# Loading q in 1 KB pieces, transposing it head by head, and reordering the first loads of an attention + FFN kernel

## The chip, the cores and the metric

The kernel runs on one core of a Trainium2 chip. The metric is the device time of one execution in microseconds. Three runs of the kernel before gave 884.79, 886.57 and 888.91 us, a median of 886.57 us.

## What is computed

The inputs are q, k and v of 8 batches, 8 heads, 576 positions and 64 features, a gain `g_norm` of 64 values, and two weight matrices of 512 x 2048 and 2048 x 512, which arrive as 64-bit floats.

```
kv  = einsum('bhsd,bhse->bhde', k, v)            # a 64 x 64 matrix for each batch and head
out = einsum('bhsd,bhde->bhse', q, kv)
x   = out / sqrt(mean(out*out, -1) + 1e-6) * g_norm   # rows: 4608 tokens, columns: 8 heads x 64
h   = x @ w_in
g   = h * tanh(log1p(exp(min(h, 20))))           # for h > 20: h * tanh(h)
result = g @ w_out                               # 4608 x 512
```

## The kernel before, in words

The 4608 tokens are nine tiles of 512. Because a batch has 576 positions, tile 0 lies in batch 0 alone, tile 1 takes 64 tokens of batch 0 and 448 of batch 1, and so on; `segments(j)` gives the pieces of a tile. In a first part each tile goes through attention and the first matrix product, and its result is stored to DRAM (`gd`); in a second part this is loaded again and multiplied with `w_out`. Both products use a seven-product scheme on 2 x 2 blocks (`PROD`), each operand as a high and a low half in a short float type, so that one product is a run of 12 matmul instructions (L527 in the first part, L772 in the second).

**Weights.** The 64-bit `w_in` is loaded in eight pieces of 1 MB, called `weights(0)` to `weights(7)`, each by two transfers (L137). A piece has to be turned into halves before a product can use it, in steps that the code names: `SCALE` (ScalarE, L142), `JOIN` (VectorE, three operations L147 to L149), `DIFF` (VectorE, L157 to L159), `BLOCKS` and `SUMS` (a cast on ScalarE, L121, and a subtraction on VectorE, L122). The raw words wait in a room that is free again after `JOIN`: pieces 0, 4 and 7 share the room `w64`, pieces 2 and 5 the room `wf6`, pieces 3 and 6 the room `wf7`.

**Attention.** For batch 0, k and v come in two halves of four heads each (L226, `kv_first`) and are multiplied in `kv_first_product` (L234). For every later batch k and v come in four parts of two heads (`k_load(b, 0)` to `k_load(b, 3)`, four transfers each: `km`, `kr`, `vm`, `vr`, L213 and L214), and `k_product(b, p)` (L252) multiplies them; only two parts have a place to land at once, so part 2 can be sent for once the product of part 0 is done. `kv_keep` copies the result out of PSUM (ScalarE, L269 and L274; VectorE, L276). A tile's heads are worked in two units of four heads. For tiles 0 and 1 a unit is: `transpose` q on TensorE (L325), copy it out (`turned`, L338 or L336), `project` with kv (L360), `square` (L370, L373), `scaled` (L378, from tile 1 on, with the gain `gcol`), `sums` (L391, L399), `rstd` (L408, L409 for tile 0) and `normalize` (L430, with `gcol`). For later tiles VectorE transposes.

**What sets the order.** The order on each engine is that of the program text; nothing is rearranged. The first tile is written out line by line. From then on a table orders the work: a step of the table, a slot, is one product of 12 matmuls, and `at(n, ...)` hangs other work behind the product of slot n. All loads and nearly all stores are issued by one engine, SyncE (SP), in program order, and an issue waits until its room is free; what stands behind it waits too. SP also keeps at most eight transfers under way: each issue waits for the landing of the one eight places earlier. After slot 0's work come, in the table: `weights(6, LOAD)` and `weights(3)` at slot 1 and `k_load(1, 2)` behind them; `k_load(1, 3)` at slot 2; `weights(4, SCALE)` and the other steps of piece 4 from slot 4; `kv_keep(1)` at slot 4; `project` of tile 1 at slots 5 and 11; the second `transpose` of tile 1 at slot 8.

Of the kernel before, what the change touches and what calls it, by code (L numbers as in the profile page):

```python
# [8 lines left out]
F32 = mybir.dt.float32  # L9
# [18 lines left out]
def linear_attention_rms_mish_ffn(  # L28
# [49 lines left out]
    G = 2 * P  # L78
# [4 lines left out]
    TR = T // P  # L83
# [11 lines left out]
    att = part1.enter_context(tc.tile_pool(name="att", bufs=1))  # L95
# [132 lines left out]
    def kv_first_product(n):  # L228
        kt, vt = kv0
        for hp in range(n.start, n.stop):  # L230
            for c in range(9):
                for o in range(2):
                    r, d = slice(o * D, (o + 1) * D), slice(c * D, (c + 1) * D)
                    nc.tensor.matmul(kvps[r, 0, hp, :], kt[r, hp, d], vt[r, hp, d], start=(c == 0), stop=(c == 8))  # L234
# [21 lines left out]
    kvf, kvt = [], []  # L256
# [9 lines left out]
    def kv_keep(b, n):  # L266
        for r in (slice(0, D), slice(D, P)):
            if b < T32:
                nc.scalar.copy(kvf[b][r, n, r], kvps[r, b % 2, n, :])  # L269
        if b < T32 - 1:  # L270
            return
        t = kvt[b % 2]
        for r in (slice(0, D), slice(D, P)):
            nc.scalar.copy(t[r, 0, n, r], kvps[r, b % 2, n, :])  # L274
        for r in (slice(0, D), slice(D, P)):
            nc.vector.tensor_sub(t[r, 1, n, r], kvps[r, b % 2, n, :], t[r, 0, n, r].bitcast(F32))  # L276


    def segments(j):

        n = (S - T) * j
        segs = []
        if n:
            segs.append((j - 1, S - n, slice(0, n)))
        if n < T:
            segs.append((j, 0, slice(n, T)))
        return segs

    def rows_load(j, c):
        for b, s0, cols in segments(j):  # L290
            t0, t1 = max(cols.start, c * P), min(cols.stop, (c + 1) * P)
            if t0 < t1:
                src = q[b, 0:1, s0 + t0 - cols.start:s0 + t0 - cols.start + 1, :]
                src = bass.AP(src.tensor, src.offset, [[D, t1 - t0], [S * D, H], [1, D]])
                nc.sync.dma_start(rows[j][t0 - c * P:t1 - c * P, c, :].rearrange("p (h d) -> p h d", d=D), src)

    rows = {}
    qs, ss = {}, {}

    def unit_steps(j, u):  # L300
        st = {}
# [13 lines left out]
        def transpose():  # L315
            if j < T32:
                if j == 0 and u == 1:
                    ps = [bank_new("a").rearrange("p m t -> p (m t)") for _ in range(2)]
                else:
                    x2 = ps_t.tile([P, 2, T], F32, name="x2")  # L320
                    ps = [x2[:, a] for a in range(2)]
                for a in range(2):
                    h = 4 * u + 2 * a
                    for c in range(TR):
                        nc.tensor.transpose(ps[a][:, c * P:(c + 1) * P], rows[j][:, c, h * D:(h + 2) * D], ident)  # L325
                st["ps"] = ps if j == 0 and u == 1 else x2
                return
            t = st["q"] = att.tile([P, 2, T], F32, name="fl")
            src = qs[u].rearrange("p a (c d) -> p (a c) d", d=D)[:, :, 0:R]
            nc.vector.transpose(t.rearrange("p a (c d) -> p (a c) d", d=R), src)  # L330
# [19 lines left out]
        def project():  # L350
            if j == 0 and u == 1:
                st["x"] = [bank_new("a").rearrange("p m t -> p (m t)") for _ in range(2)]
            else:
                x2 = st["x2"] = ps_t.tile([P, 2, T], F32, name="x2")
                st["x"] = [x2[:, a] for a in range(2)]
            for a in range(2):
                ps, hp = st["x"][a], 2 * u + a
                for b, _, c in segments(j):
                    if j < T32:
                        nc.tensor.matmul(ps[:, c], kvf[b][:, hp, :], st["q"][:, a, c], start=True, stop=True)  # L360
                        continue
                    kh, kl, qh, ql = kvt[b % 2][:, 0, hp, :], kvt[b % 2][:, 1, hp, :], st["qh"][:, a, c], st["ql"][:, a, c]
                    nc.tensor.matmul(ps[:, c], kl, qh, start=True, stop=False)
                    nc.tensor.matmul(ps[:, c], kh, ql, start=False, stop=False)
                    nc.tensor.matmul(ps[:, c], kh, qh, start=False, stop=True)
# [60 lines left out]
        def normalize():  # L426
# [39 lines left out]
    def bank_new(name):  # L466
        return ps_m.tile([P, 2, TH], F32, name=name)
# [3 lines left out]
    def at(t, f):  # L471
        plan.setdefault(t, []).append(f)
# [86 lines left out]
    def do(j, u, *steps):  # L559
        for s in steps:  # L560
            units[j][u][s]()
# [19 lines left out]
    def k_load(b, p):  # L581
        staged[b, p] = kv_load(nc.sync, b, 2 * p, 2, kv_staging())
# [5 lines left out]
    nc.scalar.preload_act_table_set("natural_log_exp_and_others")  # L588
    weights(0, LOAD)
    t = wfp.tile([P, 3, 2 * T], F32, name="wf2")  # L590
    rows[0], turned_q = t[:, 0:2].rearrange("p a (c n) -> p (a c) n", c=TR // 2), t[:, 2].rearrange("p (a t) -> p a t", a=2)
    for c in range(TR):
        rows_load(0, c)
    kv0 += [wfp.tile([P, NKC, 9 * D], F32, name=f"wf{n}") for n in (3, 4)]
    kv_first(first)
    weights(1, LOAD)
    kv_first(second)
    for r in (slice(0, D), slice(D, P)):
        nc.sync.dma_start(gcol[r, :], g_norm.rearrange("(p o) -> p o", o=1))
    weights(2, LOAD)  # L600
    weights(4, LOAD)
    weights(3, LOAD)
    make_identity(nc, ident)
    kv_tiles()
# [11 lines left out]
    do(0, 1, "transpose")  # L616
    weights(0, BLOCKS)
    do(0, 0, "turned")
    weights(0, SUMS)
    do(0, 1, "turned")  # L620
    weights(1, SCALE, JOIN)
    kv_first_product(first)
    kv_keep(0, first)
    do(0, 0, "project", "square")
    weights(1, DIFF, BLOCKS)
    kv_first_product(second)
# [4 lines left out]
    do(0, 0, "rstd")  # L631
    k_load(1, 0)
    k_load(1, 1)
    rows[1] = att.tile([P, TR, H * D], F32, name="qs")
    for c in range(TR):
        rows_load(1, c)
    do(0, 1, "square", "sums")
    weights(2, SCALE)
    do(0, 0, "normalize")
# [2 lines left out]
    do(0, 1, "rstd", "normalize")  # L642
    x_form(S1)
    weights(2, DIFF)
    weights(5, LOAD)


# [3 lines left out]
    for j in range(3, NF2):  # L651
        t = 3 * (j - 3) + 1
        if j < 5:
            at(t, lambda j=j: weights((6, 7)[j - 3], LOAD))
        for s, n in ((SCALE, 0), (JOIN, 0), (DIFF, 1), (BLOCKS, 1), (SUMS, 2)):
            at(t + n, lambda j=j, s=s: weights(j, s))

# [6 lines left out]
    for b in range(2, B):  # L664
        t = NS * (b - 2)
# [117 lines left out]
    def o_store(st):  # L783

        i, half = divmod(st["s"], T // G)
        if i < T32:
            for r in range(G // P):
                c = half * G // P + r
                for b, s0, cols in segments(i):
                    t0, t1 = max(cols.start, c * P), min(cols.stop, (c + 1) * P)  # L790
                    if t0 < t1:
                        row = b * S + s0 + t0 - cols.start
                        nc.sync.dma_start(out[row:row + t1 - t0, :], st["o"][t0 - c * P:t1 - c * P, r, :])
# [43 lines left out]
    t = NS * NT  # L837
# [13 lines left out]
    st = gs[0]  # L851
    for n in range(NF2 // 2):
        if n + 1 < NF2 // 2:
            g_pair(st, n + 1, pair_rooms(n + 1))
        for c in range(2):
# [3 lines left out]
            for (left, right), (b, h) in where.items():  # L859
                gf = st["f"][left, n]  # L860
                for s, (a, d) in enumerate(((1, 0), (0, 1), (0, 0))):
# [3 lines left out]
                        start=n == c == s == h == 0, stop=last_one, skip_group_check=True,  # L865
# [87 lines left out]
```

## Time and profile before

| quantity | value |
|---|---|
| median of 3 runs | 886.57 us |
| the profiled execution's own time | 885.97 us |
| its span, first to last instruction | 884.2 us |
| TensorE (PE) busy | 828.1 us, 94% |
| VectorE (DVE) busy | 608.7 us, 69% |
| ScalarE (ACT) busy | 464.6 us, 53% |
| PE busy in the first 54 us | 24.14 us |
| PE busy from 54 to 97 us | 39.84 of 43 us |

The page of the profile cuts the span into 40 slices of 22.1 us; a digit is the busy share in tenths. A timeline row has the start, the time from the start of the first to the end of the last instruction of the row, the engine (SPq is the queue in which SP issues transfers), the line, the operation, the tiles written and read, shapes and the count; in brackets the idle time before it and what ended that. A 32-bit float matmul shows as two matmul instructions, a transpose as one. The chain of waits follows the work that ended last back through what released it.

### The profile page before, as it was taken

Reading aid. Unit: us, or ns where it says so; the run is one execution under the profiler, and the core shown is the slowest. Engines: PE = TensorE matmul, PEld = TensorE weight load, DVE = VectorE, ACT = ScalarE, POOL = GpSimd, SP = SyncE. Lnnn points to the kernel's source line nnn. Section 1 sums busy time; section 2 is a strip of 40 time slices with the busy share of each in tenths; the row PEclk is TensorE's granted clock in tenths of the full one; section 3 lists DMA queues with packets and bytes.
Section 4 is the critical chain, followed back from the end, with each engine's and each line's share of the span. In section 5 each row is a group of like instructions: output and inputs, shape, how many; then the busy total and the mean of one; then the engine's idle time right before and its main releaser. Section 6 shows DMA issues by size and latency. Waiting matters only on the chain.

```text
span 884.2 us, 17156 instructions
## 1 busy us (share of the span) xinstructions
PE 828.1 (94%) x7036; PEld 795.7 (90%) x7036; DVE 608.7 (69%) x804; ACT 464.6 (53%) x703; POOL 4.8 (1%) x23
## 2 busy tenths in 40 slices
PE   4658998998999999999999899999999999999997
PEld 3447898998999999999999789999999999999997
DVE  5869675886777676787764368867777677776772
ACT  3647666556675765666664444344444434434431
POOL 2000000000000000000000000000000000000000
PEclk9969999999999999999999999999999999999999
DMA  9936787987978696767477993344434443334421
GB/s 294 247 114 197 200 274 246 278 263 226 296 219 278 218 304 199 220 204 227 151 227 249 425 416 125 122 150 152 148 121 133 130 120 120 119 120 141 153 65 48
DMA packets 161038, 175.52 MB, mean 199 GB/s; under 512 B 24704, under 2 KB 142464, under 8 KB 159936
## 3 DMA queue, kind: packets, MB, share of 16 engines
q1 hardware_dynamic: 158208, 170.23, 61.8%
q10 hardware_dynamic: 2752, 4.20, 1.3%
q8 instruction: 55, 0.90, 0.4%
q14 instruction: 23, 0.19, 0.1%
HBM read 112.39 MB, written 62.00 MB: 197 GB/s over the span
## 4 chain that ended last, share of the span: by engine, by line
PE 63%; DMA 11%; DVE 10%; ACT 9%; issue 4%; SPq 2%; ACTq 0%; DVEq 0%
PE a L772 22%; PE bc L772 16%; PE a L527 13%; PE bc L527 7%; DMA gd<-ula 5%; PE s L252 2%; DMA vm<-in_v_dram 2%; DVE ur L548 1%; DMA wod<-wst 1%; ACT L412 1%; ACT gf L121 1%; DMA rd<-fl 1%; DVE gf L122 1%; DVE fa L122 1%; ACT L118 1%
## 5 line engine op out<-in xcount | busy, mean ns | idle before, releaser
L772 PE MATMUL a<-wf,gf 128*128 128x256 f32 x1632 | 201.8, 283 | 0.5 <-DVE ur L812 0.5
L772 PEld LDWEIGHTS a<-wf,gf 128*128 128x128 f32 x1632 | 198.4, 192 | 0.7 <-DVE ur L812 0.7
L122 DVE TENSOR_TENSOR gf<-g,gf 128x1024 fp32r<-128x1024 f32 (+1 forms) x123 | 132.9, 1087 | 90.7 <-ACT gf L121 90.7
L527 PE MATMUL a<-gf,wf 128*128 128x256 f32 x1296 | 173.0, 287 | 11.5 <-DVE gf L430 4.5
L527 PEld LDWEIGHTS a<-gf,wf 128*128 128x128 f32 x1296 | 162.9, 193 | 18.1 <-ACT ur L504 6.6
L527 PE MATMUL bc<-gf,wf 128*128 128x256 f32 x1296 | 170.3, 285 | 3.5 <-ACT ur L495 2.4
L527 PEld LDWEIGHTS bc<-gf,wf 128*128 128x128 f32 x1296 | 161.4, 191 | 5.1 <-ACT ur L495 2.6
L121 ACT CAST gf<-g 128x1024 fp32r<-128x1024 f32 (+1 forms) x123 | 114.6, 939 | 93.3 <-DVE g L752 65.1
L772 PE MATMUL bc<-wf,gf 128*128 128x256 f32 x1224 | 152.7, 283 | 1.0 <-DVE gf L122 1.0
L772 PEld LDWEIGHTS bc<-wf,gf 128*128 128x128 f32 x1224 | 149.4, 192 | 1.4 <-ACT gf L121 0.7
L527 PE MATMUL a<-a,wf 128*128 128x256 f32 x432 | 59.8, 289 | 2.5 <-DVE ur L548 2.5
L527 PEld LDWEIGHTS a<-a,wf 128*128 128x128 f32 x432 | 55.8, 195 | 5.6 <-DVE ur L548 3.1
L118 ACT ACTIVATE ur<-ur 128x1024 f32<-128x1024 f32 x36 | 38.1, 1059 | 37.1 <-DVE ur L548 37.1
L122 DVE TENSOR_TENSOR fa<-fl,fh 128x1024 fp32r<-128x1024 f32 x28 | 34.3, 1224 | 22.1 <-ACT fh L121 21.2
L504 ACT COPY ur<-a 128x512 f32<-128x512 f32 (+1 forms) x53 | 27.3, 516 | 37.6 <-PE a L772 24.6
L122 DVE TENSOR_TENSOR gf<-gf 128x512 fp32r<-128x512 f32 x45 | 30.4, 689 | 24.0 <-ACT gf L121 24.0
L121 ACT CAST gf<-a 128x1024 fp32r<-128x1024 f32 x17 | 17.9, 1052 | 53.5 <-DVE a L749 50.9
L121 ACT CAST gf<-gf 128x512 fp32r<-128x512 f32 x45 | 27.1, 618 | 31.4 <-DVE gf L451 19.1
L495 ACT COPY ur<-bc 128x512 f32<-128x512 f32 (+1 forms) x53 | 27.4, 517 | 29.9 <-PE bc L772 23.0
L548 DVE TENSOR_TENSOR ula<-bc,ula 128x512 f32<-128x512 f32 x36 | 24.8, 688 | 25.4 <-PE bc L527 25.3
L118 ACT ACTIVATE ula<-ula 128x512 f32<-128x512 f32 x36 | 22.8, 633 | 22.1 <-DVE ula L548 22.1
L252 PE MATMUL s<-vm,km 128*64 128x64 f32 x448 | 20.1, 235 | 14.1 <-DMA vm<-in_v_dram 14.1
(137 smaller groups left out, 858.1 us busy)
## 6 DMA issues: line engine op xcount, KB each, us to landing
g<-gd SPq DMA_DIRECT2D x18, 2048.0 KB, 8.9
gd<-ur SPq DMA_DIRECT2D x32, 512.0 KB, 4.0
wod<-wst SPq DMA_DIRECT2D x16, 896.0 KB, 5.6
wf<-wod SPq DMA_DIRECT2D x8, 1792.0 KB, 16.2
gd<-ula SPq DMA_DIRECT2D x32, 256.0 KB, 5.1
gd<-ulb SPq DMA_DIRECT2D x32, 256.0 KB, 4.3
w<-in_moe_w_out_dram SPq DMA_DIRECT2D x32, 256.0 KB, 4.6
km<-in_k_dram SPq DMA_DIRECT2D x28, 256.0 KB, 4.8
```

The lines of the kernel that those rows point to most:

```text
L118: nc.scalar.activation(o, i, AF.Mish)
L121: nc.scalar.copy(hi, src)
L122: nc.vector.tensor_sub(lo, src, hi.bitcast(F32))
L252: nc.tensor.matmul(kvps[o * D:(o + 1) * D, b % 2, h0 // 2 + i, :], kt, vt, start=(c == 0), stop=(c == CM))
L412: nc.scalar.preload_act_table_set("natural_log_exp_and_others")
L495: then(t + 2, lambda: nc.scalar.copy(dst(st, "22"), st["c"]))
L504: then(t + 4, lambda: nc.scalar.copy(dst(st, "12"), st["a"]))
L527: nc.tensor.matmul(bank[:, jj], w[:, right, a, kc, :], xf[:, b, kc, :], start=first and jj == kc == s == 0, stop=(kc == 1 and s == 2), ski ...
L548: nc.vector.tensor_add(o, bank, o)
L772: nc.tensor.matmul(bank, gf[:, a, c, :], wo[c][:, right, b, :], start=first and c == s == 0, stop=(c == NF2 - 1 and s == 2), skip_group_ch ...
```

## The change

- q of tiles 0 and 1 is laid out anew: partition p holds tokens 4p to 4p+3 of the tile (before: p, 128+p, 256+p, 384+p), head by head, so that a contiguous piece in DRAM is 1 KB and no longer 256 bytes. Tile 0 needs one transfer of 1 MB (before four of 256 KB), tile 1 needs two (before five).
- The transposes of tiles 0 and 1 take one head at a time: 16 ordinary 32-bit matmuls against the identity for each unit, 128 x 64 stationary, the two heads of a pair into the two halves of the output partitions (before: 8 transposes of 128 x 128, two heads at once).
- In `project` of tile 1 the columns of a batch are now 16 or 112 in each of four groups of 128, read and written with that stride.
- The loads of later weights move: `weights(4, LOAD)` from before `weights(3, LOAD)` to the end of the first tile's text, in front of `weights(5, LOAD)`; `weights(6, LOAD)` and `weights(7, LOAD)` by two slots, behind `k_load(1, 2)` and `k_load(1, 3)`.
- `gcol` is loaded by GpSimd's queue (before by SP's).
- In the first tile's text `kv_first_product(first)` and `kv_keep(0, first)` come ahead of `weights(1, SCALE, JOIN)`, and the second unit's copy of the turned q ahead of `weights(0, SUMS)`.
- The stores of the result of tiles 0 and 1 follow the new token order: one transfer for each batch and half tile, 4 KB pieces.

```
@@ rows_load
+    def spots(cols):
+        return slice(cols.start // TR, cols.stop // TR)
-    def rows_load(j, c):
+    def rows_load(j):
         for b, s0, cols in segments(j):
-            t0, t1 = max(cols.start, c * P), min(cols.stop, (c + 1) * P)
-            if t0 < t1:
-                src = q[b, 0:1, s0 + t0 - cols.start:s0 + t0 - cols.start + 1, :]
-                src = bass.AP(src.tensor, src.offset, [[D, t1 - t0], [S * D, H], [1, D]])
-                nc.sync.dma_start(rows[j][t0 - c * P:t1 - c * P, c, :].rearrange("p (h d) -> p h d", d=D), src)
+            p = spots(cols)
+            src = q[b, 0:1, s0:s0 + 1, :]
+            src = bass.AP(src.tensor, src.offset, [[TR * D, p.stop - p.start], [S * D, H], [1, TR * D]])
+            nc.sync.dma_start(rows[j][p], src)
@@ transpose
-                    h = 4 * u + 2 * a
                     for c in range(TR):
-                        nc.tensor.transpose(ps[a][:, c * P:(c + 1) * P], rows[j][:, c, h * D:(h + 2) * D], ident)
+                        for o in range(2):
+                            src = rows[j][:, 4 * u + 2 * a + o, c * D:(c + 1) * D]
+                            nc.tensor.matmul(ps[a][o * D:(o + 1) * D, c * P:(c + 1) * P], src, ident, start=True, stop=True)
@@ project
-                        nc.tensor.matmul(ps[:, c], kvf[b][:, hp, :], st["q"][:, a, c], start=True, stop=True)
+                        o, r = (t.rearrange("p (c n) -> p c n", n=P)[:, :, spots(c)] for t in (ps, st["q"][:, a]))
+                        nc.tensor.matmul(o, kvf[b][:, hp, :], r, start=True, stop=True)
@@ the first tile's text
-    for c in range(TR):
-        rows_load(0, c)
+    rows_load(0)
...
-        nc.sync.dma_start(gcol[r, :], g_norm.rearrange("(p o) -> p o", o=1))
+        nc.gpsimd.dma_start(gcol[r, :], g_norm.rearrange("(p o) -> p o", o=1))
     weights(2, LOAD)
-    weights(4, LOAD)
     weights(3, LOAD)
...
     do(0, 0, "turned")
+    do(0, 1, "turned")
     weights(0, SUMS)
-    do(0, 1, "turned")
-    weights(1, SCALE, JOIN)
     kv_first_product(first)
     kv_keep(0, first)
+    weights(1, SCALE, JOIN)
...
-    for c in range(TR):
-        rows_load(1, c)
+    rows_load(1)
...
     weights(2, DIFF)
+    weights(4, LOAD)
     weights(5, LOAD)
@@ the table
         if j < 5:
-            at(t, lambda j=j: weights((6, 7)[j - 3], LOAD))
+            at(t + 2, lambda j=j: weights((6, 7)[j - 3], LOAD))
```

The order on SP, in the rows that follow the loads of tile 1's q (`qs`). `wf_387` is weights(5) and `wf_441` weights(6) before; `w_394` is weights(4), `wf_397` weights(5) and `wf_540` weights(6) in the change. Before:

```order
L295 DMA qs<-in_q_dram 128x8x64 x3
L137 DMA wf_387<-in_moe_w_in_dram 128x4x256 x2
L137 DMA wf_441<-in_moe_w_in_dram 128x4x256 x2
L213 DMA km<-in_k_dram 128x2x256
L214 DMA kr<-in_k_dram 64x2x64
L213 DMA vm<-in_v_dram 128x2x256
L214 DMA vr<-in_v_dram 64x2x64
```

In the change:

```order
L298 DMA qs<-in_q_dram 112x8x256
L137 DMA w_394<-in_moe_w_in_dram 128x4x256 x2
L137 DMA wf_397<-in_moe_w_in_dram 128x4x256 x2
L213 DMA km<-in_k_dram 128x2x256
L214 DMA kr<-in_k_dram 64x2x64
L213 DMA vm<-in_v_dram 128x2x256
L214 DMA vr<-in_v_dram 64x2x64
L213 DMA km<-in_k_dram 128x2x256
L214 DMA kr<-in_k_dram 64x2x64
L213 DMA vm<-in_v_dram 128x2x256
L214 DMA vr<-in_v_dram 64x2x64
L137 DMA wf_540<-in_moe_w_in_dram 128x4x256 x2
```

weights(6) now stands behind all eight transfers of batch 1's third and fourth parts, and weights(4) and weights(5) stand ahead of them.

The order on ScalarE in the first tile's text, from the copy of the first turned q on (`wf_217`/`wf_227` are weights(0) as halves, `wf_148`/`wf_145` the raw words of weights(1), `kvf` the kept kv of batch 0). Before:

```order
L338 COPY fh<-x_198 128x1024
L121 CAST wf_217<-wd 128x4x256
L142 ACTIVATE fl<-wf_148 128x1024
L269 COPY kvf_168<-s_123 64x2x64 x2
L370 ACTIVATE fa<-x_271 128x1024
```

In the change:

```order
L342 COPY fh<-x_192 128x1024
L121 CAST wf_227<-wd 128x4x256
L269 COPY kvf_162<-s_123 64x2x64 x2
L142 ACTIVATE fl<-wf_145 128x1024
L375 ACTIVATE fa<-x_281 128x1024
```

The copies of the first kv product moved ahead of the scaling of weights(1).

More of the change, by code (lines that the diff above doesn't have):

```diff
@@ L590, in linear_attention_rms_mish_ffn @@
     t = wfp.tile([P, 3, 2 * T], F32, name="wf2")
-    rows[0], turned_q = t[:, 0:2].rearrange("p a (c n) -> p (a c) n", c=TR // 2), t[:, 2].rearrange("p (a t) -> p a t", a=2)
-    for c in range(TR):
-        rows_load(0, c)
+    rows[0], turned_q = t[:, 0:2].rearrange("p a (h n) -> p (a h) n", h=H // 2), t[:, 2].rearrange("p (a t) -> p a t", a=2)
+    rows_load(0)
     kv0 += [wfp.tile([P, NKC, 9 * D], F32, name=f"wf{n}") for n in (3, 4)]
@@ L633, in linear_attention_rms_mish_ffn @@
     k_load(1, 1)
-    rows[1] = att.tile([P, TR, H * D], F32, name="qs")
-    for c in range(TR):
-        rows_load(1, c)
+    rows[1] = att.tile([P, H, TR * D], F32, name="qs")
+    rows_load(1)
     do(0, 1, "square", "sums")
@@ L786, in o_store @@
         if i < T32:
[L787 to L793, printed above, removed]
+            for b, s0, cols in segments(i):
+                p = spots(cols)
+                row = b * S + s0 + half * G // P
+                dst = out[row:row + 1, :]
+                dst = bass.AP(dst.tensor, dst.offset, [[TR * DM, p.stop - p.start], [DM, G // P], [1, DM]])
+                nc.sync.dma_start(dst, st["o"][p])
             return
```

## The prediction

> **What bounds the kernel now.** I read the page first, then the list of waits, then the timelines of the engines that these name.
>
> ```profile
> span 884.2 us, 17156 instructions
> PE   4658998998999999999999899999999999999997
> PEclk9969999999999999999999999999999999999999
> km<-in_k_dram SPq DMA_DIRECT2D x28, 256.0 KB, 4.8
> ```
>
> TensorE is busy nine tenths from the fifth slice on; whatever the change gains or loses there is its own work. The room is in the first three slices (4, 6, 5), 66 us, where all edits lie but the stores. Who waits for whom from 54 us on, and then SP's, ScalarE's and VectorE's timelines:
>
> ```profile
> PE s L252 <- DMA vm<-in_v_dram: 12.9, 1, 12.9
> ```
>
> ```profile
> 35.19 12.57 SPq L137 DMA_DIRECT2D wf<-in_moe_w_in_dram  x4
> 47.86 0.45 SPq L213 DMA_DIRECT2D km<-in_k_dram  x1
> 49.06 0.59 SPq L213 DMA_DIRECT2D vm<-in_v_dram  x1
> ```
>
> ```profile
> 50.31 1.04 ACT L121 CAST wf<-wd 128x1024 fp32r<-128x1024 f32 x1
> 59.05 0.58 ACT L504 COPY ur<-a 128x512 f32<-128x512 f32 x1 [7.70 <-PE a L527]
> 59.53 1.12 ACT L142 ACTIVATE fl<-w 128x1024 f32<-128x1024 f32 x1
> 70.58 1.11 ACT L378 ACTIVATE gf<-x,gcol 128x1024 f32<-128x1024 f32 x1
> ```
>
> ```profile
> 32.29 1.23 DVE L149 SCALAR_TENSOR_TENSOR fl<-wf,fl 128x1024 uint32<-128x1024 uint32 x1
> 51.73 1.22 DVE L122 TENSOR_TENSOR wf<-wd,wf 128x1024 fp32r<-128x1024 f32 x1
> 60.69 0.69 DVE L147 TENSOR_SCALAR fl<-fl 128x1024 uint32<-128x1024 uint32 x1 [7.74 <-ACT fl L142]
> ```
>
> TensorE stands 12.9 us for part 2 of batch 1's k and v. SP is held from 35.19 to 47.76 by four issues, of weights(5) and weights(6); the latter waits for a room that VectorE's third join of weights(3) frees. Only then are k and v sent for. But VectorE and ScalarE used that time: they converted weights(3) until 51.73 + 1.22 = 52.95 and 50.31 + 1.04 = 51.35. Their own loss is 7.74 and 7.70 us. And the next stretch is theirs:
>
> ```profile
> 58.95 0.69 PE L252 MATMUL s<-vm,km 128*64 128x64 f32 x16
> 62.78 2.12 PE L360 MATMUL x<-fh,kvf 128*128 128x64 f32 x8
> 71.75 1.22 PE L325 MATMUL x<-ident,qs 128*128 128x128 f32 x8 [2.54 <-ACT gf L378]
> 72.62 2.91 PE L527 MATMUL a<-a,wf 128*128 128x256 f32 x12
> 77.52 1.69 PE L527 MATMUL a<-gf,wf 128*128 128x256 f32 x12
> ```
>
> At 71.75 TensorE waits once more, 2.54 us, for ScalarE's L378, which ends a chain of conversions that began with the scaling of weights(4) at 59.53. So what reaches the end is how much earlier that scaling starts, not how long TensorE stood.
>
> **The change part by part.**
>
> *Moved loads: +7.70 us.* weights(4) needs nothing (its room's first tenant is joined by then) and weights(5) waits for the third join of weights(2), 32.29 + 1.23 = 33.5. Part 2 then waits for its place, that is for the product of part 0 (36.47 + 1.12 in a row below, with the rest by 37.9), and not for 47.86. Its four issues take 0.45 to 0.60 each, so vm is issued near 39.1 and, with 4.8 us to landing as on the page, is there by 43.9. Part 3 follows the product of part 1 (its last start near 40.5): issued 40.8 to 43, there by 47. TensorE then does part 2 (1 us), the third product (1.6, or 2.9 at the slow clock) and is done by 47.7 at the latest. ScalarE wants this product at 51.35. So its whole wait of 7.70 goes, with 3.6 us in hand; `kv_keep(1)` wants part 3's product near 53, with 4 us in hand. What is late next is ScalarE itself: TensorE will stand for `kv_keep` and then again for L378, some 3 us each. Less than 7.70 comes out only if part 2 lands after 47.5. Weights(4) to (7) land later than now, but weights(4) is wanted at 51, weights(5) near 60; weights(6) is issued after the third join of weights(3) as now, weights(7) after that of weights(4) as now: nothing.
>
> *Start: +0.85 us.* Here are the rows, DMA stretches first (the last number is GB/s), then TensorE, ScalarE and VectorE.
>
> ```profile
> 0.00:4.00 4.00, 0.00 (x0) 0.00 (x0) 0.00 (x0) 1.28 (x1) 3.40 (x12) 1.00 0.47 143
> 6.00:9.00 3.00, 0.72 (x2) 0.36 (x2) 1.47 (x2) 1.12 (x1) 0.00 (x0) 1.00 1.39 219
> 20.00:24.00 4.00, 4.00 (x77) 2.74 (x76) 3.86 (x7) 2.61 (x6) 0.00 (x0) 1.00 1.09 356
> ```
>
> ```profile
> 12.11 1.91 PE L325 MATMUL a<-ident,wf 128*128 128x128 f32 x8
> 14.35 2.39 PE L234 MATMUL s<-wf,wf 64*64 64x64 f32 x72 [0.32 <-DMA wf<-in_v_dram]
> 24.89 1.88 PE L360 MATMUL a<-wf,kvf 128*128 128x512 f32 x4
> 36.47 1.12 PE L252 MATMUL s<-vm,km 128*64 128x64 f32 x16
> ```
>
> ```profile
> 17.32 1.12 ACT L142 ACTIVATE fl<-wf 128x1024 f32<-128x1024 f32 x1 [3.01 <-DMA wf<-in_moe_w_in_dram]
> 18.34 0.51 ACT L269 COPY kvf<-s 64x128 f32<-64x128 f32 x2
> 23.75 1.05 ACT L121 CAST wf<-wd 128x1024 fp32r<-128x1024 f32 x1
> ```
>
> ```profile
> 22.90 0.42 DVE L159 TENSOR_TENSOR wd<-fl,wd 128x256 f32<-128x256 f32 x1
> 27.21 1.41 DVE L430 SCALAR_TENSOR_TENSOR gf<-x,gcol,fa 128x512 f32<-128x512 f32 x2 [1.15 <-ACT fa L409]
> ```
>
> The 256-byte pieces of q move at 219 GB/s, larger ones at 356. weights(0) and q are 2.1 MB; at 356, from about 2.4 us (0.57 MB by 4.0), they are in at 8.3, when the transposes begin; the first k and v (1.2 MB) follow by 11.7 and no longer set the start of their product.
>
> The new transposes do. Their price is in no row; the nearest is L252, also 128 x 64 stationary with alternating output halves. With a last instruction of 0.22 (0.31 slow) its 16 start every (0.69 - 0.22)/15 = 31 ns, (1.12 - 0.31)/15 = 54 ns at the slow clock. L360 streams 512 columns in (1.88 - 0.59)/3 = 0.43 us, 54 ns for 64: so two halves overlap in L252. Twice the columns make 62 ns (slow 108) if they overlap here too, 108 (slow 215) if not. I take the overlap. The instruction lengths show which clock holds when:
>
> ```profile
> L325 PE MATMUL a<-ident,wf x8: 421/421/422, 12.1 to 13.6; 128*128 128x128 f32 x8
> ```
>
> ```profile
> L325 PE MATMUL x<-ident,qs x16: 272/273/404, 40.6 to 72.6; 128*128 128x128 f32 x16
> ```
>
> ```profile
> L360 PE MATMUL a<-wf,kvf x4: 592/593/593, 24.9 to 26.2; 128*128 128x512 f32 x4
> ```
>
> ```profile
> 31.60:35.00 3.40, 0.77 (x6) 0.77 (x7) 3.33 (x5) 0.32 (x1) 0.00 (x0) 1.00 0.86 193
> 35.10:38.40 3.30, 3.30 (x29) 2.84 (x29) 3.20 (x7) 0.62 (x1) 0.00 (x0) 0.50 1.28 221
> 72.60:75.90 3.30, 3.30 (x16) 2.74 (x14) 3.16 (x7) 2.25 (x6) 0.00 (x0) 0.50 0.58 162
> ```
>
> TensorE is slow up to 14.5, and stretches of 3.4 us are slow after one in which it stood (0.77 busy, then 0.50). Of 64 transposes from 8.3, if the clock lifts at 12.0, 34 run slow and 30 fast: done at 13.9. If it lifts at 11.1, 13.5; at 14.6, 15.0. The Trainium skill (TensorE: Matmul & The Clock Gate, section "What's actually happening") calls the activity window free-running, so that the count of slow matmuls changes from run to run; by it any point from 13.5 to 15.0 is as good.
>
> The first kv product (2.39) ends at 16.3, its copies (0.51, now ahead of weights(1)) at 16.9. L142 starts there, not at 17.32, and VectorE's L159 ends 6.0 later (22.90 + 0.42 - 17.32), at 22.9. The cast that now starts at 23.75, held by the copies of the second kv product, starts with it: 0.85 us earlier (1.35 to -0.15), and all up to 51.35 is in order behind it. The second product is no brake: project at 17.0, then 1.9 and 2.3, ends at 21.2.
>
> *Transposes in tile 1: -1.1 us.* The first unit's lie in front of part 2's landing and cost nothing; without that cover, 1.1. The second unit's begin when L378 lets them: 32 x 62 ns = 2.0 in place of 72.62 - 71.75 = 0.87. From there TensorE is the bound. The slow stretch after the standing (2.91 for a product that takes 1.69 otherwise) is there now and will be again; bounds -0.6, and -2.6 without overlap.
>
> The Trainium skill (TensorE: Matmul & The Clock Gate, section "Measured speedup vs the span model") gives three column tiles 2.38 times one, an efficiency of 0.79. For two that is an estimate of 1.6 times, 68 ns in place of 62: start and second unit would lose 0.4 together, sum 7.0. L252's own 54 against 31 is 1.74 times, and I keep it.
>
> *At nothing.* `gcol` by GpSimd: first read by L430 at 27.21, some 20 us after GpSimd is free; if it held the identity beyond 8.3, the start would pay. The strided columns of `project` are as many as now (2.12 us for eight; at worst again as much in each unit, mostly covered). Stores of tiles 0 and 1: fewer issues on SP in the second part, behind TensorE. q of tile 1 now follows the first two parts directly behind weights(3), 1 MB earlier in the queue, and is wanted only behind the product of part 1.
>
> **Sum**: 7.70 + 0.85 - 1.1 = 7.45. The profiled execution took 885.97, so 878.5; it lies 0.6 below the median of 886.57, so I leave it at that. Its own range is 876.8 to 880.5.
>
> **Rivals.**
>
> *The output halves do not overlap.* 17 slow and 47 fast of 108 ns end at 17.1; the cast slips 2.2, the second unit costs 2.6: 7.70 - 4.8 = 2.9, 883.1. For it: these are full-height weights and twice L252's columns; against it L252.
>
> *Slower: they neither overlap nor wake the clock.* The place is the start and the second unit. 64 x 215 ns end at 22.1, the cast at 31.0 (7.2 late), the second unit pays 6.0: 885.97 + 5.5 = 891.5. It decides from 157 ns for an instruction on, where 96 of them eat the 7.70. For it: the slow clock held up to 14.5 although transposes ran since 7.6. Against it: it lifted at the end of an unbroken stretch of them.
>
> *The load does not come earlier*, because SP is held at weights(5) or by its limit of eight as long as now: only the other terms stay, 885.97 - 0.85 + 1.1 = 886.2. Against it: the third join of weights(2) ends at 33.5.
>
> *More*: the clock lifts at 11.1 and the slow stretch of 2.91 against 1.69 falls elsewhere, 0.5 + 1.2 more: 876.8 or a little less.
>
> **How the numbers follow.** Forecast 0.62, no overlap 0.11, slower 0.05, load not earlier 0.08, more 0.14. A measurement tells some 0.5%, 4.4 us, from no change. Forecast and more are faster beyond that: 0.76. No overlap (3.5 below the median) and the late load are within it: 0.19. Slower: 0.05. The range 874.5 to 884.0 takes in the first, second and last case and leaves out 0.13 and some tail.
>
> **What would show it.** Right: no wait of L252 over 2 us near 42; ScalarE's L504 without a wait; L378 8 to 9 us earlier; a second unit of 2 us. Wrong: L142 of weights(1) after 18; transposes over 100 ns each at the full clock; vm issued after 44.

## The result, and the profile after

The change took 882.08 us (median of 5, 881.72 to 882.62) against 886.57 us before (median of 5, 884.79 to 892.07): the ratio is 0.9942, with a 95% interval of 0.9916 to 0.9968. That is 4.5 us less. The forecast was 878.5, so 3.6 us of the expected gain did not come. The profiled execution took 882.62 us with a span of 880.8; before, the span was 884.2.

The first lines of the page of the change, which answer to those shown of before:

```profile
span 880.8 us, 17335 instructions
...
PE   4679998989999999999999799999999999999997
...
PEclk9999999999999999999999999999999999999999
...
q0 software_dynamic: 64, 0.00, 0.0%
```

The third slice of TensorE rises from 5 to 7; the first two are as they were (4, 6). The last line is new: a queue with 64 packets and no megabytes to speak of, GpSimd's load of `gcol`.

TensorE's timeline of the change, from the first transposes on:

```profile
12.01 3.68 PE L329 MATMUL x<-ident,wf 128*64 128x128 f32 x32 [12.01 <-DMA wf<-in_q_dram]
15.45 2.66 PE L329 MATMUL a<-ident,wf 128*64 128x128 f32 x32
18.05 2.31 PE L234 MATMUL s<-wf,wf 64*64 64x64 f32 x72
...
43.98 1.97 PE L329 MATMUL x<-ident,qs 128*64 128x128 f32 x32
45.82 0.69 PE L252 MATMUL s<-vm,km 128*64 128x64 f32 x16
46.43 0.33 PE L252 MATMUL s<-vr,kr 64*64 64x64 f32 x4
46.70 1.69 PE L532 MATMUL a<-gf,wf 128*128 128x256 f32 x12
48.54 0.69 PE L252 MATMUL s<-vm,km 128*64 128x64 f32 x16 [0.15 <-DMA vm<-in_v_dram]
...
56.93 2.86 PE L365 MATMUL x<-fh,kvf 128*128 128x448 f32 x6 [3.01 <-ACT kvf L269]
58.91 4.49 PE L532 MATMUL a<-gf,wf 128*128 128x256 f32 x24
63.23 1.60 PE L532 MATMUL bc<-gf,wf 128*128 128x256 f32 x12
67.33 2.95 PE L329 MATMUL x<-ident,qs 128*64 128x128 f32 x32 [2.50 <-ACT gf L383]
70.21 2.29 PE L532 MATMUL a<-a,wf 128*128 128x256 f32 x12
72.42 1.88 PE L404 MATMUL ss<-fa,sel 128*8 128x512 f32 x4
```

The wait of 12.9 us for part 2 is gone: its product follows at 45.82 without a wait, and part 3's at 48.54 with one of 0.15 us. In its place stand two waits for ScalarE, 3.01 and 2.50 us, as forecast. But the first row is the surprise: q is in at 12.01, where the forecast had 8.3, and the transposes end near 18.1, not at 13.9. The second unit's transposes, from 67.33 to 70.21, took 2.9 us and not 2.0.

ScalarE's timeline of the change:

```profile
20.46 0.53 ACT L269 COPY kvf<-s 64x128 f32<-64x128 f32 x2 [2.77 <-PE s L234]
21.02 1.14 ACT L142 ACTIVATE fl<-wf 128x1024 f32<-128x1024 f32 x1
27.08 1.04 ACT L121 CAST wf<-wd 128x1024 fp32r<-128x1024 f32 x1 [0.29 <-DVE wd L159]
...
53.68 1.05 ACT L121 CAST wf<-wd 128x1024 fp32r<-128x1024 f32 x1
54.63 0.58 ACT L509 COPY ur<-a 128x512 f32<-128x512 f32 x1
55.11 1.14 ACT L142 ACTIVATE fl<-w 128x1024 f32<-128x1024 f32 x1
...
66.17 1.11 ACT L383 ACTIVATE gf<-x,gcol 128x1024 f32<-128x1024 f32 x1
```

The copy of the product (L509, L504 before) starts without a wait; the 7.70 us are gone. The cast at 27.08 is the one that stood at 23.75 before: the start has lost 3.33 us. 7.70 - 3.33 = 4.37, and the scaling of weights(4) stands 4.42 us earlier than before (55.11 against 59.53), L383 4.41 earlier (66.17 against 70.58).

This cast of weights(1) is a good place to cut the span. Up to it runs the start; from it to the end everything else. Before: 23.75 + 860.4 = 884.2. Change: 27.08 + 853.8 = 880.8. **The part behind the cut gained 6.7 us, where the forecast had 7.70 - 1.1 = 6.6. The start lost 3.3, where it had a gain of 0.85.** The whole miss lies in the first 27 us.

How fast the transfers moved there, in the windows of one microsecond of the change (the last two numbers are the mean busy share of the 16 DMA engines and GB/s):

```profile
4.00:5.00 1.00, 0.00 (x0) 0.00 (x0) 0.00 (x0) 0.00 (x0) 1.00 (x2) 1.00 1.06 359
5.00:6.00 1.00, 0.00 (x0) 0.00 (x0) 0.00 (x0) 0.00 (x0) 0.94 (x4) 1.00 0.88 248
6.00:7.00 1.00, 0.00 (x0) 0.00 (x0) 0.00 (x0) 0.00 (x0) 0.72 (x7) 1.00 0.65 168
7.00:8.00 1.00, 0.00 (x0) 0.00 (x0) 0.00 (x0) 0.58 (x1) 0.41 (x5) 1.00 0.86 283
8.00:9.00 1.00, 0.00 (x0) 0.00 (x0) 0.43 (x1) 0.54 (x1) 0.00 (x0) 1.00 1.03 343
```

From 5 to 8 us the rate falls to 248, 168 and 283 GB/s, and the engines are not even busy (0.65 in the middle row). In the trace GpSimd's 64 packets run from 4.4 to 9.3 us, just there. That is a coincidence in time only; the runs below test it.

### The profile page after: what moved, and what is told of

Same layout as the page of the kernel before. It is cut to its first block, busy times and chain, and to the rows that moved or that the text cites. A ratio compares the mean times of both kernels' runs of the same rounds, so it can differ in the third digit from the quotient of the medians.

```text
span 880.8 us, 17335 instructions
## 1 busy us (share of the span) xinstructions
PE 833.6 (95%) x7132; PEld 801.7 (91%) x7132; DVE 608.3 (69%) x804; ACT 464.8 (53%) x703; POOL 6.0 (1%) x25
## 4 chain that ended last, share of the span: by engine, by line
PE 63%; DMA 10%; ACT 10%; DVE 9%; issue 4%; SPq 2%; ACTq 0%; DVEq 0%
PE a L775 22%; PE bc L775 16%; PE a L532 12%; PE bc L532 7%; DMA gd<-ula 5%; PE s L252 2%; DMA wod<-wst 1%; DMA wf<-in_q_dram 1%; DVE ur L553 1%; ACT L417 1%; ACT gf L121 1%; DVE gf L122 1%; DMA w<-in_moe_w_out_dram 1%; DMA rd<-fl 1%; DVE fa L122 1%
## 5 line engine op out<-in xcount | busy, mean ns | idle before, releaser
L509 ACT COPY ur<-a 128x512 f32<-128x512 f32 (+1 forms) x53 | 27.4, 516 | 30.8 <-PE a L775 24.6
L118 ACT ACTIVATE ula<-ula 128x512 f32<-128x512 f32 x36 | 22.8, 633 | 22.5 <-DVE ula L553 22.5
L553 DVE TENSOR_TENSOR ur<-bc,ur 128x512 f32<-128x512 f32 x36 | 24.4, 677 | 9.0 <-PE bc L532 6.0
```

Of the source, the lines that this page charges most:

```text
L118: nc.scalar.activation(o, i, AF.Mish)
L509: then(t + 4, lambda: nc.scalar.copy(dst(st, "12"), st["a"]))
L553: nc.vector.tensor_add(o, bank, o)
```

## The experiments

The medians are of 5 or 6 runs (12 for g_norm by GpSimd in the kernel before). The kernels ran in three groups, each beside the kernel before on the same chip, and from one group to another only the ratio to it carries over. Its median was 887.65 us in the first group (17 runs; g_norm on SP, g_norm by GpSimd in the kernel before, only the moved loads, q ahead of weights(0)), 886.6 in the second (9 runs; the change again, g_norm on SP again, weights(1) early, loads and order) and 886.16 in the third (11 runs; the other four).

First the summary, by the cut at the cast of weights(1). "Rest" is the span, before it is rounded, less that start.

| kernel | median us | ratio to before, 95% | first transpose | cast of weights(1) | span | rest |
|---|---|---|---|---|---|---|
| before | 886.57 | | 7.59 | 23.75 | 884.2 | 860.4 |
| before, g_norm by GpSimd | 888.35 | 1.0018 [1.0003, 1.0033] | 7.97 | 24.68 | 885.4 | 860.8 |
| before, loads moved | 879.49 | 0.9923 [0.9902, 0.9945] | 7.47 | 23.87 | 877.1 | 853.3 |
| the same, and text reordered | 878.34 | 0.9914 [0.9901, 0.9928] | 7.58 | 23.14 | 876.4 | 853.2 |
| that again | 880.22 | 0.9925 [0.9904, 0.9946] | 7.76 | 25.91 | 879.3 | 853.4 |
| change, g_norm on SP, tile 1 as before | 879.48 | 0.9929 [0.9909, 0.9949] | 9.30 | 24.56 | 877.8 | 853.2 |
| change, g_norm on SP | 880.52 | 0.9924 [0.991, 0.9938] | 9.43 | 23.76 | 877.1 | 853.4 |
| that again | 880.21 | 0.9926 [0.9914, 0.9939] | 10.67 | 24.98 | 879.0 | 854.0 |
| that a third time | 880.43 | 0.9935 [0.9919, 0.9952] | 10.41 | 25.91 | 881.0 | 855.1 |
| change, g_norm by GpSimd, late | 879.93 | 0.9928 [0.9912, 0.9944] | 10.57 | 25.48 | 879.1 | 853.7 |
| change, g_norm on SP, q ahead of weights(0) | 879.39 | 0.9917 [0.9903, 0.9932] | 6.92 | 24.00 | 878.0 | 854.0 |
| change, g_norm on SP, weights(1) early | 880.47 | 0.9923 [0.991, 0.9935] | 9.69 | 23.67 | 878.9 | 855.3 |
| the change | 882.08 | 0.9942 [0.9916, 0.9968] | 12.01 | 27.08 | 880.8 | 853.8 |
| the change again | 882.04 | 0.9951 [0.9938, 0.9965] | 11.86 | 25.94 | 880.0 | 854.1 |

### g_norm back on SP

```
-        nc.gpsimd.dma_start(gcol[r, :], g_norm.rearrange("(p o) -> p o", o=1))
+        nc.sync.dma_start(gcol[r, :], g_norm.rearrange("(p o) -> p o", o=1))
```

> The change with one part undone: g_norm is loaded by SP again, at its old place. Theory A (GpSimd's two small transfers of g_norm slowed the transfers of weights(0) and q between 5 and 8 us, where the changed kernel moved 168 to 283 GB/s in place of some 360): q lands near 8.6 and not at 11.9, the transposes start there, the scaling of weights(1) starts near 17.1 and not at 21.0, and the time falls by 3.3 to 3.9 us to some 878.5. Theory B (one transfer of 1 MB, whose landing waits for the slowest of 16 engines, is itself what lands late): q lands near 11.9 as in the change and the time stays at 882.

It took 880.52 us, some 2 us more than the theory's 878.5. q is in at 9.43 instead of 12.01, and the stretch from 5 to 8 us moves 308, 355 and 315 GB/s. So g_norm's way may have to do with it, but one execution of each is not enough: the landing of q could differ from execution to execution. The two were therefore timed beside each other on one chip.

> The changed kernel once more, beside the same with g_norm on SP, on one chip. Theory A (the small transfers of g_norm from GpSimd's queue hold back some of the 16 engines): in a second profile q again lands late, near 11.9, and the time is 3.3 us over that of the kernel with g_norm on SP, as their first profiles have it (second transposes of tile 1 at 67.3 and 64.1). Rival (the lateness differs from execution to execution, the profiled one was a bad draw): q lands between 9.5 and 11.5, and the two medians are 1 to 2 us apart.

> The change with g_norm on SP once more: by Theory A 3.3 us under the changed kernel beside it, by its rival 1 to 2 us; q lands near 9.3 by both.

882.04 against 880.21 us: 1.8 us for g_norm by GpSimd. The rival was right about the size, 1.8 and not 3.3, and about the spread: the same kernel had q in at 9.43 and at 10.67. But the change's own 12.01 and 11.86 lie above both, and the slowest of the five runs with g_norm on SP, 880.87, lies below the fastest of the five with GpSimd, 881.5.

### g_norm by GpSimd in the kernel before

> The kernel before with this one part of the change done: g_norm by GpSimd. Theory A: the stretch from 5 to 8 us moves less, the landings of q and of the first v slip by 1.3 us (the bytes that were missing in the change, 0.49 MB at 360 GB/s) to 2.8 us (the slowest engine's lag there), the first kv product starts that much after 14.35, and the time rises to between 887.9 and 889.4. Theory B: nothing moves at the start, 886.6, or less by the 1 us that SP and the transfers save near 19 us.

The edit is the one above, reversed, in the kernel before. The ratio is 1.0018 with an interval of 1.0003 to 1.0033: a loss, and a small one, 0.7 us. There the 64 packets took 2.4 us (4.5 to 6.9), the transposes began 0.4 us later and the first kv product 0.9 us later. So the price is not fixed.

### g_norm by GpSimd, but later

GpSimd first copies one column of q into `gcol`, so that its transfer must wait until q has landed:

```
+    nc.gpsimd.tensor_copy(gcol, rows[0][:, 0, 0:1])
+    for r in (slice(0, D), slice(D, P)):
+        nc.gpsimd.dma_start(gcol[r, :], g_norm.rearrange("(p o) -> p o", o=1))
```

> The change with g_norm still by GpSimd, but sent for only after q of tile 0 has landed (GpSimd first copies one column of q into gcol, and the transfer has to wait for this copy). Theory 1 (GpSimd's small packets cost because they run beside weights(0) and q): q lands as with g_norm on SP, transposes begin at 9.4 to 10.7 us, and the median is within 0.7 us of that kernel (880.2 to 880.9). Rival (a transfer by GpSimd costs wherever it stands, since it sets the 16 engines apart for all later transfers): the first transposes begin as early, but weights(1) and with it the scaling of weights(1) comes 1 to 2 us late, and the median is 1.5 to 2 us above that kernel, near 882.

> The change with g_norm on SP's queue, a third time, as the neighbour of the three kernels beside it. From the two earlier executions: 880.2 to 880.5 us, first transposes begin between 9.4 and 10.7 us.

879.93 us, and 880.43 for its neighbour with g_norm on SP: no difference. GpSimd's and TensorE's rows of the late one:

```profile
10.57 0.18 POOL L615 COPY gcol<-wf 128x1 f32<-128x1 f32 x1 [4.68 <-DMA wf<-in_q_dram]
11.09 1.17 POOL L617 DMA_DIRECT2D gcol<-in_g_norm_dram  x2 [0.34 <-POOL gcol L615]
```

```profile
10.57 3.68 PE L329 MATMUL x<-ident,wf 128*64 128x128 f32 x32 [10.57 <-DMA wf<-in_q_dram]
14.01 2.51 PE L329 MATMUL a<-ident,wf 128*64 128x128 f32 x32
```

and its windows of one microsecond:

```profile
5.00:6.00 1.00, 0.00 (x0) 0.00 (x0) 0.00 (x0) 0.00 (x0) 0.61 (x7) 1.00 0.97 305
6.00:7.00 1.00, 0.00 (x0) 0.00 (x0) 0.00 (x0) 0.67 (x1) 0.00 (x0) 1.00 1.03 347
7.00:8.00 1.00, 0.00 (x0) 0.00 (x0) 0.52 (x1) 0.44 (x1) 0.00 (x0) 1.00 1.07 369
```

The dip of 168 GB/s is gone, although the queue and its 64 packets are the same. Sent late, all 64 pass within 0.8 us (15.4 to 16.2); sent early, they took 5.0 us. So the place in time costs, not GpSimd's queue as such, and the rival that it costs wherever it stands falls. What holds the engines idle while the early packets trickle through is not in the trace: in the change a packet itself takes 9 to 11 ns, and 64 of them over 16 engines are nothing. Company alone does not do it, since the late packets passed beside loads of 375 GB/s. Two differences remain untested: the early packets ran beside weights(0) and q, and they ran while GpSimd still filled constant tiles (2.41 to 7.59 us in the change).

The trace shows how far the early delay reaches. Each of these transfers lands in 16 shares, one for each DMA engine. In the change the last share of q came 2.8 us after the first (9.06 and 11.88), and every later load up to the one that landed at 22.44 kept this distance of 2.8 to 2.9 us. So not only q came late, but k, v and weights(1) behind it. That it is the same engine each time is likely but not shown, since the landings do not name their engine. With g_norm on SP the distance for q was 0.6, 1.9 and 1.8 us in the three executions, and it stayed within 0.1 of that up to 18 us.

### Only the moved loads, in the kernel before

```
-    weights(4, LOAD)
     weights(3, LOAD)
...
     weights(2, DIFF)
+    weights(4, LOAD)
     weights(5, LOAD)
...
-            at(t, lambda j=j: weights((6, 7)[j - 3], LOAD))
+            at(t + 2, lambda j=j: weights((6, 7)[j - 3], LOAD))
```

> The kernel before with the loads of weights(4), weights(6) and weights(7) moved as in the change and nothing else. Theory of the prediction (the moved loads alone give back ScalarE's wait of 7.70 us, all else is start and transposes): the wait of L504 for TensorE goes, the second transposes of tile 1 start 7.7 us earlier at 64.0, and the time is 886.6 - 7.7 = 878.9. Rival (the gain of the moved loads needs q in 1 KB pieces as well, since q of tile 1 in 256-byte pieces holds SP and the engines until 37.9): parts 2 and 3 of batch 1 land after 47.5, half or more of the wait stays, 882.5 or more.

879.49 against 887.65 us: the theory holds, and the rival that q must come in 1 KB pieces as well falls. TensorE and ScalarE of this kernel:

```profile
44.38 0.69 PE L252 MATMUL s<-vm,km 128*64 128x64 f32 x16 [1.41 <-DMA vm<-in_v_dram]
...
53.71 3.61 PE L360 MATMUL x<-fh,kvf 128*128 128x448 f32 x6 [2.66 <-ACT kvf L269]
...
64.13 1.97 PE L325 MATMUL x<-ident,qs 128*128 128x128 f32 x8 [2.45 <-ACT gf L378]
```

```profile
51.41 0.58 ACT L504 COPY ur<-a 128x512 f32<-128x512 f32 x1
51.89 1.14 ACT L142 ACTIVATE fl<-w 128x1024 f32<-128x1024 f32 x1
```

The second unit begins 7.62 us earlier (71.75 - 64.13), the scaling of weights(4) 7.64 (59.53 - 51.89): the forecast's 7.70, to a tenth. In the table the rest falls from 860.4 and 860.8 to 853.3, which is 7.3. Moving these loads is alone as good as any kernel here; which of the moves, that of weights(4) or that of weights(6) and weights(7), gives how much was not tested.

### q ahead of weights(0)

```
-    weights(0, LOAD)
     t = wfp.tile([P, 3, 2 * T], F32, name="wf2")
     ...
     rows_load(0)
+    weights(0, LOAD)
```

(on the change with g_norm on SP)

> The change with g_norm on SP again and with q of tile 0 sent for ahead of weights(0). If Theory A holds and the landing of q sets the start: q lands near 5.5, weights(0) near 8.7, the transposes are done by 11.5, the first kv product waits for v near 12, the scaling of weights(1) starts near 16.8 (ScalarE does the casts of weights(0) first), 4.2 us before the changed kernel's, and the time is 877.9. Rival (the conversion of weights(0), now 1.5 us later, sets the start): the scaling of weights(1) starts no earlier than in the kernel without this move, 878.5 or more.

It took 879.39 us; its neighbour with g_norm on SP took 880.52, and the runs of the two overlap. q is in at 6.92, 2.5 us earlier than with weights(0) ahead of it, and the transposes end at 11.94. The cast of weights(1) stays where it was, at 24.00 (23.76 there). ScalarE tells why:

```profile
9.88 1.16 ACT L142 ACTIVATE fl<-w 128x1024 f32<-128x1024 f32 x1 [7.85 <-DMA w<-in_moe_w_in_dram]
14.32 0.92 ACT L121 CAST wf<-fl 128x256 fp32r<-128x256 f32 x2 [3.28 <-DVE fl L149]
15.15 1.00 ACT L342 COPY fh<-x 128x1024 f32<-128x1024 f32 x1
16.06 1.04 ACT L121 CAST wf<-wd 128x1024 fp32r<-128x1024 f32 x1
17.00 0.53 ACT L269 COPY kvf<-s 64x128 f32<-64x128 f32 x2
17.56 1.15 ACT L142 ACTIVATE fl<-wf 128x1024 f32<-128x1024 f32 x1
```

weights(0) is scaled 3.7 us later (9.88 for 6.14), its casts take ScalarE from 14.32 to 17, and the copies and L142 queue behind them. The rival was right: with q earlier, the conversion of weights(0) sets the start. Trading the places of these two loads gained nothing that can be told.

### weights(1) ahead of the first kv product, as before

```
+    weights(1, SCALE, JOIN)
     kv_first_product(first)
     kv_keep(0, first)
-    weights(1, SCALE, JOIN)
```

(and the second copy of the turned q behind `weights(0, SUMS)` again; on the change with g_norm on SP)

> The change with g_norm on SP and with the reordering of the first tile's text undone: weights(1) is scaled and joined ahead of the first kv product and its copies again, and the casts of weights(0) ahead of the copy of the second turned q. Theory (in the change the reordering costs: weights(1) has landed by 15.3, but its scaling now waits for the product and starts at 17.7): the scaling starts at 15.4, the cast of weights(1)'s differences near 22.5 in place of 23.8, and the time is 1.2 us under that of the kernel with g_norm on SP alone. Rival (the reordering helps, as it did in the prediction's sum: the copies come 1 us later without it): the cast stays at 23.8 or later, no gain or a loss of up to 1 us.

880.47 against 880.21 us for its neighbour: no difference. L142 came at 15.68 as expected, but the cast at 23.67, not 22.5. VectorE had its own queue in front of the joins:

```profile
15.39 1.23 DVE L122 TENSOR_TENSOR wf<-wd,wf 128x1024 fp32r<-128x1024 f32 x1 [2.15 <-ACT wf L121]
16.54 1.28 DVE L340 COPY wf<-a 128x512 f32<-128x512 f32 x2
17.73 0.69 DVE L147 TENSOR_SCALAR fl<-fl 128x1024 uint32<-128x1024 uint32 x1
```

The first join could start at 17.73 only, 0.9 us after L142 had ended, and then the copies of the second kv product (23.11) stood before the cast. 23.67 lies at the early end of the 23.76 to 25.91 that the kernel without this edit showed in three executions, and the median did not move: no gain from the order of these lines can be told either way.

### The loads and the order, without the new layout of q

The kernel before with the moved loads and the reordered text of the first tile, nothing else.

> The kernel before with the moved loads and the reordering of the first tile's text, but q in 256-byte pieces with the old transposes and g_norm on SP. Theory (in the old layout weights(1) lands at 17.3 and the first product ends near 16.9, so that the copies need no longer wait for weights(1)): project starts at 17.5 in place of 19.1, the second product waits for v until 20.5, the cast of weights(1)'s differences starts 0.4 us earlier at 23.4, and the time is 0.4 us under that of the moved loads alone (879.5), 879.1. Rival (the q layout is needed for any gain at the start): no difference. Either way this kernel less the one with g_norm on SP tells what the layout of q is worth: by the traces so far 1.4 us of it are lost in the transposes of tile 1, so it should be slower by 1 us than this one.

878.34 us, 1.9 below the change with g_norm on SP on the same chip. This looked like the price of q's layout, so it was run a second time, and beside it a kernel that keeps the new layout for tile 0 and gives tile 1 its old one.

> The kernel before with the moved loads and the reordered first tile's text, a second time, on the chip of the three kernels beside it: 878.3 us, 1.9 below the change with g_norm on SP's queue. If it comes out within 0.7 of that kernel here, the price of q's new layout was one chip's.

> The change with g_norm on SP's queue and with q of tile 1 as in the kernel before (five transfers of 256-byte pieces, transposes of two heads, stores in the old token order); q of tile 0 stays new. Theory (most of what the new layout costs, 1.9 us, lies in the second unit of tile 1): from the second unit's transposes to the first product of sums takes 2.5 to 4.0 us instead of 5.1, and the median is 1.1 to 2.0 us lower than with the change's tile 1, 878.2 to 879.1. Rival (it lies at the start): no difference within 0.5 us.

On this chip the three came out at 880.22 (old layout), 879.48 (new for tile 0 alone) and 880.43 (new). The 1.9 us do not hold. The second execution of the old layout shows what else moves, on TensorE:

```profile
12.19 1.91 PE L325 MATMUL a<-ident,wf 128*128 128x128 f32 x8
15.15 4.05 PE L234 MATMUL s<-wf,wf 64*64 64x64 f32 x72 [1.05 <-DMA wf<-in_v_dram]
```

The first kv product waited 1.05 us for v, and then ran at the slow clock: 4.05 us, where it took 2.31 in the first execution. The cast of weights(1) stands at 25.91 instead of 23.14. So the same program's start differs by 2.8 us, and the old layout, whose transposes have finished earlier, can lose that time to v and the clock.

Behind the cut the picture is steady. Four kernels with the old tile 1 have a rest of 853.2 to 853.4; eight with the new one have 853.4 to 855.3, 854.2 on average. The new layout of tile 1 costs 0.9 us there, all of it together: loads, transposes, `project` in strides and stores. So the theory of this pair holds in the trace, though at half the expected size; by the times, 879.48 against 880.43, the difference lies within the intervals. The new tile 0 (879.48) and the old one (880.22) cannot be told apart.

## Why the prediction was right or wrong

**Right in sign and range, too low by 3.6 us; the step that failed lies at the start.** That the time fell into the range does not bear out the start: the range reached to 884.0 to take in the rival without overlap, and 882.08 lies nearer to that rival's 883.1 than to the forecast.

*Moved loads, +7.70: right.* Alone they gave 7.62 and 7.64 at two places of the timeline, 7.3 in the rest of the span. That ScalarE's own wait and not TensorE's 12.9 us was the measure is what made the number: 5.2 of the 12.9 would have been a false gain. Part 2 was sent for at 41.33 and not 37.9, since the start was late, and its product and the third one behind it were done by 48.4; ScalarE wanted them at 54.63, so 6 us were in hand where the forecast had 3.6. That TensorE's standing is not the measure shows also in the first execution of the loads and the order without the new layout. There TensorE still stood 4.45 us for part 2, ScalarE's L504 at 50.67 had no wait, and the rest was 853.2 as in the others:

```profile
45.60 1.12 PE L252 MATMUL s<-vm,km 128*64 128x64 f32 x16 [4.45 <-DMA vm<-in_v_dram]
```

*Overlap of the output halves: right.* At the full clock the 32 instructions from 43.98 begin 57.5 ns apart, (45.82 - 43.98)/32; the forecast had 62. With the first 32 at the start they take 3.44/32 = 108 ns (15.45 - 12.01), the forecast's number for the slow clock. The Trainium skill (TensorE: Matmul & The Clock Gate, section "Measured speedup vs the span model") has 2.38 times for three column tiles. The estimate of 68 ns that was worked out from it was too careful for two halves: 57.5 against the 108 without overlap is 1.88 times. The forecast's doubt that these weights are full-height set nothing apart from L252, whose shape in the rows is 128*64 too.

*Transposes in tile 1, -1.1: near in size, by other means than forecast.* By the rests the new layout of tile 1 cost 0.9. But the second unit's transposes were priced at the full clock, 2.0 us, and took 2.88 in the change, since some 20 of the 32 fell into a slow stretch ((2.88 - 32 x 0.0575)/0.05). From the unit's first transpose to the first product of `sums` the change took 72.42 - 67.33 = 5.1 us and the kernel before 3.7; over all profiled executions it is 5.0 to 6.1 us with the new layout of tile 1 and 2.5 to 4.0 with the old one. Part of this is won back behind it. That the total is near 1.1 is luck in part.

*Start, +0.85: the step that failed*, with "`gcol` by GpSimd: at nothing". Three things are in it:

- **g_norm by GpSimd cost 1.8 us.** The prediction looked at when GpSimd would be free and who reads `gcol`, and both were harmless: the identity was done by 3.0, and the first reader of `gcol` had stood at 27.21. It did not ask what a transfer in another queue does to the transfers that the start waits for. The condition it named ("if it held the identity beyond 8.3, the start would pay") was the wrong one.
- **q was in at 9.3 to 10.7 even without that, not at 8.3.** The bytes moved about as forecast (in the late one 305 to 386 GB/s from 5 to 9 us), but one transfer of 1 MB is done only when the last of the 16 engines has its share. In the trace q's shares ended 0.6 us apart where it was in at 9.4 and 1.9 apart where it was in at 10.7, and already the eighth of the 16 was in only at 8.9 in all three executions with g_norm on SP. So 8.3 by a mean rate was 0.6 us early for the middle share, and the transposes wait for the last one. What follows q was sized well: from q to the cast of weights(1) it took 14.3, 14.3 and 15.5 us there, where the forecast had 22.9 - 8.3 = 14.6.
- **The start does not follow q alone.** q at 6.92 instead of 9.43 left the cast where it was, and L142 at 15.68 instead of 18.93 left the median where it was: conversion of weights(0), VectorE's queue and v wait just behind. The forecast moved one brake by 0.85 us, while the same program's start differs by up to 2.8 us between executions.

Measured term by term: 7.3 (loads) - 0.9 (layout of tile 1) - 1.8 (g_norm) + 0 (start otherwise, not told from nothing) = 4.6, and the change gained 4.5. The first two terms come from single profiled executions and the third from medians, so the agreement to 0.1 is luck in part.

*Rivals.* "No overlap" would have given 883.1, close to what came, and is still wrong: the instruction distances rule it out. "Not earlier" and "slower" fell with L252's and the transposes' rows, and "more" (876.8) did not come. Without the trace the time alone would have picked the wrong one.

*The signs named for right and wrong* told the truth: L252's wait, L504, the transposes at full clock and `vm` issued at 42.45 spoke for; L142 of weights(1) at 21.02, behind the 18 named as wrong, and L383 earlier by 4.4 us and not by 8 to 9, spoke against the start, and a second unit of 2.9 us and not 2 against its price.

*The better version.* The kernel before with the moved loads, with or without the reordered text, took 878.3 to 880.2 us; so did the change with g_norm on SP or late (879.9 to 880.5). No run tells these apart. On the one chip where the change ran again beside three of them, they lay 1.6 to 3.7 us below it.

## What to carry to other kernels

Where an engine stands for a late load, the gain from an earlier one is the idle time of the engine that sets the pace behind it, here ScalarE's 7.7 us and not TensorE's 12.9. A small transfer that nobody needs soon can still have a price at the start: here it cost 1.8 us beside the first two loads and nothing behind them, on the same queue. And a forecast of a start that several loads and engines reach within a microsecond of each other should take a gain there as zero until a trace shows which is last.

## What the runs showed of the hardware

- Two transfers of 64 numbers by GpSimd, 64 packets of 16 and 4 bytes and 9 to 11 ns each, took 5.0 and 4.9 us to pass while weights(0) and q were loading (the two executions of the change), 2.4 us beside the 256-byte pieces of before, and 0.8 us sent at 11 us. In the first case the large transfers ran at 168 to 289 GB/s from 5 to 8 us, where they ran at 305 to 369 with the load sent late; the DMA engines were busy 62 to 94% of that time, and the shares of q on the 16 engines ended 2.6 to 2.8 us apart.
- A lag between the shares of a load stays for the loads behind it: in the change the last share came 2.8 to 2.9 us after the first from q to the load that landed at 22.44; in the two later executions with g_norm on SP it came 1.7 to 1.9 us after it, from q to the loads that landed near 20 us.
- 128 x 64 stationary matmuls of 128 columns that alternate between the two halves of the output begin every 56 to 58 ns at the full clock and every 107 to 108 ns at the slow one.
- When the clock lifts differs between executions of one program: the second 32 transposes of the start took 1.93, 1.93 and 3.08 us in the three executions with g_norm on SP. The Trainium skill (TensorE: Matmul & The Clock Gate, section "What's actually happening") has the activity window run free of the program; that agrees with these rows.
